# Decoding float64 weights on VectorE alone by a shorter formula, with every split of the experts' weights on VectorE

## The chip, the cores and the metric

The kernel runs on one core of a Trainium2 chip. The metric is device time in microseconds (us) of one execution; less is better. The names of the engines: PE is TensorE (PEld is its weight load), DVE is VectorE, ACT is ScalarE, POOL is GpSimd, SP is SyncE, which here only issues DMAs.

## The reference, cut to what matters

Three layers follow one another: a gated linear attention, a mixture of eight experts in which each token goes to one expert, and a dense feed-forward layer with a leaky ReLU.

```python
# attention, for every batch and head, over S = 768 steps
state = f[:, :, t, :, None] * state + einsum('bhd,bhe->bhde', k[:, :, t], v[:, :, t])
y[:, :, t] = einsum('bhd,bhde->bhe', q[:, :, t], state)
# x: 3072 tokens x 384
expert_idx = argmax(x @ w_gate, axis=1)          # 8 experts
h = maximum(xe @ w1[e], 0.0); ye = h @ w2[e]     # w1: 384 x 1024, w2: 1024 x 384, per expert
out[mask] = gate_w[mask, None] * ye
# dense layer
h = x @ w_in                                     # 384 x 2048, float64
g = maximum(0.01 * h, h)
return (g @ w_out).astype(float32)               # 2048 x 384, float64
```

The weights of the dense layer, w_in and w_out, arrive as float64: they alone are drawn without a cast to float32. The chip's engines compute in float32, so the kernel takes each float64 apart as two 32-bit integer words and builds a float32 value from them.

## The kernel before

**Stages.** The attention runs first and scatters the tokens by expert. The experts follow as nine passes p = 0 to 8 of eight steps each; a step n = 8p + j handles one 128-column block of an expert's first layer and the same block of its second. Pass 0 runs the first 224 tokens of one expert while the attention is finishing, pass 1 runs 256 more of the same expert, and passes 2 to 8 run the other seven experts with room for 464, 440, 420, 408, 396, 384 and 368 tokens. The dense layer comes last: 96 steps of a first product (line 919) and a second one (line 940).

**Products in two parts.** Every float32 operand is split into a high part in the float32r format and the low remainder. `split` (line 132) does that with a ScalarE cast (line 133) and a subtraction on an engine that its caller names (line 134). A product is three matmuls per 128 rows: high by high, high by low, low by high.

**A step of the experts** is written out in the loop over n from line 874 on; the order of this loop is the order of every engine's own queue. In it `m1(n)` issues 9 matmuls of the first layer (line 296), the ReLU cast on ScalarE (line 299) and the low part `hT` on VectorE (line 300). One part of a decode comes next (`decode_on`, line 883), the DMA of weight block n + 3 (`wload`, tile `wraw`, three buffers), and then `m2(n - 1)`, 9 matmuls of the second layer (line 311). In steps 4, 5 and 6 of a pass `m_tr` transposes a third of the next expert's tokens (line 282) and splits them into `xT` (line 286, VectorE). `wsplit(n + 2)` splits the weight block: half 0 is w1's and half 1 is w2's. Half 0 has its subtraction on VectorE and half 1 on GpSimd, by the default `e1=nc.gpsimd`. Another part of a decode closes the step (line 903).

**Decoding.** A block of the float64 weights is 128 x 384 values; there are 16 of w_in and 16 of w_out. `decode(i)` is a generator of four parts, in lines 686 to 711. `decode_all` chains the 32 blocks. `decode_on` places 104 of the 128 parts, which is 26 blocks, in 109 places: two per step from step 16 on, the start of pass 2. The rest, 24 parts, go into the dense layer, two per step. The high word of a float64 is `hw`, the low word `lw`; both are read with a stride of two words. Seven instructions on VectorE make the leading bits `a` and the scaled rest `b`. For w_in a ScalarE cast and two GpSimd instructions turn these into a high and a low part (lines 709 to 711), and for w_out one GpSimd addition makes a float32 value (line 706), which is split later in the dense layer by `wosplit` (line 948, subtraction on GpSimd). The tiles `d_t`, `d_a` and `d_s` have one buffer each, and `raw` has two; the DMA of block i + 1 (`fload`) is issued in the second part of block i.

Of the kernel before, what the change touches and what calls it, by code (L numbers as in the profile page):

```python
# [7 lines left out]
FP32 = mybir.dt.float32  # L8
# [3 lines left out]
U32 = mybir.dt.uint32  # L12
ACTF = mybir.ActivationFunctionType
ALU = mybir.AluOpType
# [17 lines left out]
FB = FF // 128  # L32
# [40 lines left out]
def kernel(  # L73
# [12 lines left out]
    nc = tc.nc  # L86
# [45 lines left out]
    def split(hi, lo, src, eng):  # L132
        nc.scalar.copy(out=hi, in_=src)  # L133
        eng.tensor_tensor(out=lo, in0=src, in1=hi.bitcast(FP32), op=ALU.subtract)  # L134
# [105 lines left out]
    def wload(n, src=None, eng=nc.sync):  # L240
        if src is None:
            p, j = expert_of(n)
            if p == 1 and j < KEPT:
                return
            if p < 2:
                src = wpk[0, SECOND[j] if p else j]
            else:
                if j == 0:
                    e_at[p] = nc.values_load(tab[0:1, ORD, p - 1:p], engines=[SP_E], min_val=0, max_val=NE - 1)
                src = wpk[bass.ds(e_at[p], 1), j].rearrange("o p c -> (o p) c")  # L250
        wraw[n] = mw.tile([128, 768], FP32, tag="wraw", name="wraw")
        eng.dma_start(out=wraw[n], in_=src)

    def wsplit(n, *halves, e1=nc.gpsimd):
        if KF <= n < KF + KEPT and n not in wraw:
            return
        for i in halves or (0, 1):
            r = wraw[n] if i == 0 else wraw.pop(n)
            w = mw.tile([128, 2, 384], FP32R, tag=f"w{i}", name=f"w{i}")
            split(w[:, 0, :], w[:, 1, :], r[:, 384 * i:384 * (i + 1)], e1 if i else nc.vector)  # L260
            wsp.setdefault(n, []).append(w)

    def pieces(rows):
# [51 lines left out]
    def attention():  # L315
        with ExitStack() as st:
# [62 lines left out]
            def load(g, a=0, b=FW + 2 * SEG):  # L379
                for h in range(2):  # L380
                    nc.sync.dma_start(out=fkqb[g % NBUF][64 * h:64 * h + D, a:b], in_=fkq[g, h, :, a:b])

            def load_v(g):
                vt[g] = sb.tile([128, PB, 2, D], FP32, tag="v", name="v", bufs=7)
                nc.sync.dma_start(out=vt[g], in_=v[g])
# [35 lines left out]
            def sc(g):  # L421
                aps[g] = a = [bank(B_A + h, [PB, 128], "A") for h in range(2)]
                for p in range(PB):
                    for h in range(2):
                        r = slice(64 * h, 64 * h + 64)
                        nc.tensor.matmul(out=a[h][:, p, :], lhsT=kh[g][r, cols(p)], rhs=qh[g][r, cols(p)],
                                         start=True, stop=True)
# [10 lines left out]
            def tr(g):  # L438
                t_ps = bank(B_T, [PB, 128], "T")
                for p in range(PB):  # L440
                    nc.tensor.transpose(t_ps[:, p, :], kh[g][:, cols(p)], ident)
                kn[g] = sb.tile([128, PB, 128], FP32, tag="kn", name="kn", bufs=2)
                nc.scalar.copy(out=kn[g], in_=t_ps)
# [53 lines left out]
            def route2(i, n=2):  # L497
                route_b(i, n, bank(B_R, [n, NE], "R"))
# [38 lines left out]
            for g in range(NG):  # L537
                if g + 5 < NG:
                    load(g + 5)
                if g + 3 < NG:  # L540
                    load_v(g + 3)
                if 14 <= g < 17:
                    wload(g - 14)
                if g < 12:
                    for _ in range(2 if g % 3 == 2 else 1):
                        e, r0 = divmod(nz * ZR, GW)
                        nc.sync.dma_start(
                            out=xs[e * NT + r0:e * NT + r0 + ZR, :].rearrange("(p j) d -> p (j d)", p=128), in_=zero)
                        nz += 1
                sc(g)  # L550
                if g % NCH < NCH - 1:
                    tr(g)
                if g + 2 < NG:
                    suffix(g + 2)
                if g == 0:
                    warm_up(WARM2)
                if g + 3 < NG:
                    prep_a(g + 3)
                mask(g)
                if g >= 4:  # L560
                    logits(g - 4)
                if g >= 1 and (g - 1) % NCH < NCH - 1:
                    kv(g - 1)
                if g + 2 < NG:
                    prefix(g + 2)
                if g in (7, 11, 15, 19):
                    route_a(g - 7, 4)
                if g in (21, 23):
                    route_a(g - 5, 2)
                if g in (8, 12, 16, 20):  # L570
                    route2(g - 8, 4)
                    ready += 4
                if g == 22:
                    route2(16)
                    ready += 2
                if g == 1:
                    ys(0)
                if g > 2:
                    ys(g - 2)
                if g == 2:  # L580
                    xo(0)
                if g > 3:
                    xo(g - 3)
                out_to = ngt
                if ngt < ready:
                    gated(ngt, 2)
                    ngt += 2
                if 17 <= g < 23 and g % 2:
                    wsplit((g - 17) // 2, e1=nc.vector)
                if g == 22:  # L590
                    ok1 = check_decay()
                if g == 20:
                    wload(3)
                if g == 21:
                    wload(4)
                for _ in range(2):
                    if g >= 13 and nsc < out_to:
                        scatter(nsc)
                        nsc += 1
# [30 lines left out]
            gated(NG - 2, 2)  # L630
            scatter(NG - 2)
            scatter(NG - 1)
            wsplit(3, 1, e1=nc.vector)
            wload(6)
            e2(1)
            wsplit(4)
# [25 lines left out]
    def experts_and_ffn(place):  # L662
        with ExitStack() as st:
# [4 lines left out]
            wi = [wb.tile([128, 2, 384], FP32R, name=f"wi{i}") for i in range(FB)]  # L668
            wo = [wb.tile([128, 384], FP32, name=f"wo{i}") for i in range(FB)]
# [8 lines left out]

            def decode(i):

                r = raw.pop(i).rearrange("p (n t) -> p n t", t=2)
                lw, hw = r[:, :, 0], r[:, :, 1]
                t = dec.tile([128, 384], I32, tag="d_t", name="d_t")
                a = dec.tile([128, 384], I32, tag="d_a", name="d_a")
                s = dec.tile([128, 384], I32, tag="d_s", name="d_s")
                nc.vector.tensor_scalar(out=t, in0=hw, scalar1=0x7FF00000, scalar2=None, op0=ALU.bitwise_and)  # L686
                nc.vector.tensor_scalar(out=t, in0=t, scalar1=float(896 << 20), scalar2=float(896 << 20),
                                        op0=ALU.max, op1=ALU.subtract)
                nc.vector.tensor_scalar(out=s, in0=hw, scalar1=-0x80000000, scalar2=None, op0=ALU.bitwise_and)  # L689
                yield  # L690
                if 2 <= i + 1 < 2 * FB:
                    fload(i + 1)
                nc.vector.scalar_tensor_tensor(out=a, in0=hw, scalar=0xFFFFF, in1=t,  # L693
                                               op0=ALU.bitwise_and, op1=ALU.bitwise_or)
                nc.vector.scalar_tensor_tensor(out=a, in0=a, scalar=3, in1=s,  # L695
                                               op0=ALU.logical_shift_left, op1=ALU.bitwise_or)
                nc.vector.scalar_tensor_tensor(out=s, in0=t, scalar=3, in1=s,
                                               op0=ALU.logical_shift_left, op1=ALU.bitwise_or)
                yield
                b = t.bitcast(FP32)  # L700
                nc.vector.scalar_tensor_tensor(out=b, in0=lw.bitcast(U32), scalar=2.0 ** -52, in1=s.bitcast(FP32),  # L701
                                               op0=ALU.mult, op1=ALU.mult)
                yield
                af = a.bitcast(FP32)
                if i >= FB:
                    nc.gpsimd.tensor_tensor(out=wo[i - FB], in0=af, in1=b, op=ALU.add)
                else:
                    hi, lo = wi[i][:, 0, :], wi[i][:, 1, :]
                    nc.scalar.copy(out=hi, in_=af)
                    nc.gpsimd.tensor_tensor(out=af, in0=af, in1=hi.bitcast(FP32), op=ALU.subtract)  # L710
                    nc.gpsimd.tensor_tensor(out=lo, in0=af, in1=b, op=ALU.add)
                yield

            def decode_all():
# [342 lines left out]
```

## Time and profile before

| quantity | value |
|---|---|
| median of 3 runs | 836.73 us (836.01 to 838.64) |
| the profiled execution | 834.25 us, its span 832.5 us |
| PE busy | 778.9 us, 94% of the span |
| DVE busy | 548.2 us, 66% |
| ACT busy | 397.2 us, 48% |
| POOL busy | 352.9 us, 42% |
| granted TensorE clock, mean | 0.988 |

The span runs from the first to the last instruction; the profiled execution's own time is 1.75 us more. Busy shares are means over stages that have different limits, so a share of the whole span does not tell what one stage waits for. A matmul's busy time includes its passage through the array, so that a PE that looks fully busy may still be issuing at less than its best rate; the distance between the starts of successive groups of matmuls tells that rate.

### The profile page before, as it was taken

What the parts mean: (1) busy time and instruction counts of PE and PEld (TensorE: products, weight loads), DVE (VectorE), ACT (ScalarE), POOL (GpSimd) and SP (SyncE); (2) the same over time, 40 slices, a digit from 0 to 9 for tenths busy, and PEclk for the clock granted to TensorE, in tenths of its full rate; (3) what the DMA queues carried; (4) which work ended last, traced back from release to release, by engine and by line L of the source; (5) the groups of instructions that cost most, each with busy time, mean ns of one, the idle gap of its engine ahead of it and who ended that gap; (6) DMA issues with size and microseconds to landing.
All of it is one profiled execution on the core that took longest, in us unless ns stands there. A gap on an engine that the chain in (4) does not pass through costs nothing.

```text
span 832.5 us, 14166 instructions
## 1 busy us (share of the span) xinstructions
PE 778.9 (94%) x5201; PEld 705.8 (85%) x5202; DVE 548.2 (66%) x973; ACT 397.2 (48%) x798; POOL 352.9 (42%) x338
## 2 busy tenths in 40 slices
PE   6998988989999998999799999999999999999993
PEld 5777766889898987999789899999999999999993
DVE  7999998675898899999968843433433433343331
ACT  3666775645455444545343444434444444444441
POOL 6221562337676766666533352233224224224222
PEclk9999999999999999999999999999999999999997
DMA  9999941256476764786301010000001001001001
GB/s 188 244 281 313 260 151 40 102 181 199 149 190 131 206 160 126 210 190 152 117 31 44 20 39 1 1 17 21 1 1 39 1 1 38 1 1 39 1 0 43
DMA packets 35024, 81.78 MB, mean 98 GB/s; under 512 B 7904, under 2 KB 15168, under 8 KB 34944
## 3 DMA queue, kind: packets, MB, share of 16 engines
q1 hardware_dynamic: 31104, 71.32, 32.5%
q0 software_dynamic: 3840, 9.45, 3.1%
q8 instruction: 43, 0.70, 0.4%
q14 instruction: 37, 0.30, 0.1%
HBM read 65.02 MB, written 15.74 MB: 97 GB/s over the span
## 4 chain that ended last, share of the span: by engine, by line
PE 58%; DVE 23%; DMA 7%; issue 5%; ACT 3%; POOL 2%; POOLq 0%; SPq 0%; DVEq 0%; ACTq 0%
PE h L919 22%; PE oacc L940 22%; PE acc L311 6%; PE h L296 5%; DMA fkq<-in_fkq 5%; DVE w L134 3%; DVE d_t L686 2%; DVE kh L405 2%; DVE d_s L689 2%; DMA xs<-zero 2%; DVE d_a L695 2%; DVE d_a L693 2%; DVE hT L300 1%; DVE d_t L701 1%; DVE am L433 1%
## 5 line engine op out<-in xcount | busy, mean ns | idle before, releaser
L940 PE MATMUL oacc<-wos,g 128*128 128x384 f32 x1152 | 217.4, 337 | 0.0
L919 PE MATMUL h<-ysp,wi 128*128 128x512 f32 x864 | 213.3, 392 | 0.3 <-DVE t L928 0.3
L134 POOL TENSOR_TENSOR wos<-wo,wos 128x384 fp32r<-128x384 f32 x96 | 100.3, 1045 | 262.4 <-ACT wos L133 262.4
L940 PEld LDWEIGHTS oacc<-wos,g 128*128 128x128 f32 x1152 | 204.7, 188 | 7.8
L919 PEld LDWEIGHTS h<-ysp,wi 128*128 128x128 f32 x864 | 161.1, 188 | 28.3 <-DVE t L928 0.6
L928 DVE TENSOR_TENSOR t<-t,h 128x512 f32<-128x512 f32 (+1 forms) x97 | 66.2, 682 | 145.3 <-ACT t L927 145.3
L311 PE MATMUL acc<-hT,w 128*128 128x224 f32 (+8 forms) x648 | 125.6, 336 | 9.2 <-DVE hT L300 8.7
L296 PE MATMUL h<-xT,w 128*128 128x256 f32 (+7 forms) x576 | 118.2, 347 | 5.9 <-DVE w L134 5.8
L311 PEld LDWEIGHTS acc<-hT,w 128*128 128x128 f32 x648 | 109.1, 189 | 15.7 <-DVE hT L300 12.6
L134 DVE TENSOR_TENSOR g<-t,g 128x512 fp32r<-128x512 f32 (+1 forms) x97 | 66.7, 687 | 66.1 <-PE oacc L940 47.3
L296 PEld LDWEIGHTS h<-xT,w 128*128 128x128 f32 x576 | 98.7, 189 | 12.8 <-DVE w L134 9.8
L927 ACT ACTIVATE t<-h 128x512 f32<-128x512 f32 (+1 forms) x97 | 57.5, 592 | 103.7 <-PE h L919 103.6
L133 ACT CAST g<-t 128x512 fp32r<-128x512 f32 (+1 forms) x97 | 59.8, 617 | 94.0 <-DVE t L928 94.0
L134 POOL TENSOR_TENSOR w<-wraw,w 128x384 fp32r<-128x384 f32 x65 | 73.8, 1136 | 55.6 <-ACT w L133 54.9
L133 ACT CAST w<-wraw 128x384 fp32r<-128x384 f32 x138 | 66.8, 513 | 31.6 <-PE acc L311 23.5
L408 POOL TENSOR_TENSOR kh<-fkq,kh 128x512 f32<-128x512 f32 x24 | 28.6, 1192 | 82.0 <-DVE kh L405 44.6
L134 DVE TENSOR_TENSOR w<-wraw,w 128x384 fp32r<-128x384 f32 x73 | 58.1, 800 | 6.2 <-ACT w L133 6.2
L299 ACT ACTIVATE hT<-h 128x256 fp32r<-128x256 f32 (+7 forms) x64 | 31.9, 499 | 54.4 <-PE h L296 54.1
L133 ACT CAST wos<-wo 128x384 fp32r<-128x384 f32 x96 | 49.1, 512 | 9.1 <-PE oacc L940 0.4
L300 DVE SCALAR_TENSOR_TENSOR hT<-h,hT 128x256 fp32r<-128x256 f32 (+7 forms) x64 | 35.7, 557 | 8.7 <-ACT hT L299 8.7
L483 PE MATMUL X<-cw_sb,yt 128*128 128x104 f32 x192 | 27.6, 289 | 14.1 <-DVE lg L492 8.2
L483 PEld LDWEIGHTS X<-cw_sb,yt 128*128 128x128 f32 x192 | 23.7, 195 | 19.0 <-DVE lg L492 8.9
(139 smaller groups left out, 919.3 us busy)
## 6 DMA issues: line engine op xcount, KB each, us to landing
wraw<-in_wpk SPq DMA_DIRECT2D x69, 384.0 KB, 4.0
fkq<-in_fkq SPq DMA_DIRECT2D x44, 288.9 KB, 8.6
xs<-zero SPq DMA_DIRECT2D x16, 384.0 KB, 8.5
raw<-in_w_in SPq DMA_DIRECT2D x16, 384.0 KB, 3.9
raw<-in_w_out SPq DMA_DIRECT2D x16, 384.0 KB, 3.7
v<-in_v SPq DMA_DIRECT2D x24, 192.0 KB, 8.2
xw<-xs SPq DMA_DIRECT2D x5, 768.0 KB, 5.7
xw<-xs SPq DMA_DIRECT2D x2, 576.0 KB, 6.9
```

What stands on the lines that cost most here:

```text
L133: nc.scalar.copy(out=hi, in_=src)
L134: eng.tensor_tensor(out=lo, in0=src, in1=hi.bitcast(FP32), op=ALU.subtract)
L296: nc.tensor.matmul(out=h_ps, lhsT=w[:, a, kk * 128:(kk + 1) * 128], rhs=xT[p][kk][:, b, :], start=(kk == 0 and a + b == 0), stop=(kk == 2 ...
L299: nc.scalar.activation(out=t[:, 0, :], in_=h_ps, func=ACTF.Relu)
L300: nc.vector.scalar_tensor_tensor(out=t[:, 1, :], in0=h_ps, scalar=0.0, in1=t[:, 0, :].bitcast(FP32), op0=ALU.max, op1=ALU.subtract)
L311: nc.tensor.matmul(out=a_ps[d], lhsT=w[:, a, d * 128:(d + 1) * 128], rhs=t[:, b, :], start=(j == 0 and a + b == 0), stop=(j == KF - 1 and ...
L408: nc.gpsimd.tensor_tensor(out=tokens(kh[g]), in0=chunks(kb[g % NBUF]), in1=tokens(kh[g]), op=ALU.mult)
L483: nc.tensor.matmul(out=x_ps[:, p, :], lhsT=yt[i % 2][:, p, :], rhs=cw_sb[:, p, :], start=True, stop=True)
L919: nc.tensor.matmul(out=h_ps, lhsT=wi[i][:, a, kk * 128:(kk + 1) * 128], rhs=ysp[j][kk][:, b, :], start=(kk == 0 and a + b == 0), stop=(kk ...
L927: nc.scalar.activation(out=t[:, c], in_=h_ps[:, c], func=ACTF.Copy, scale=0.01)
L928: nc.vector.tensor_tensor(out=t[:, c], in0=t[:, c], in1=h_ps[:, c], op=ALU.max)
L940: nc.tensor.matmul(out=oacc[j][s], lhsT=g[:, b, s * 128:(s + 1) * 128], rhs=w[:, a, :], start=(i == 0 and a + b == 0), stop=(i == FB - 1 a ...
```

## The change

All of a block's decoding, apart from one ScalarE cast for w_in, moves to VectorE, by another formula. The absolute bits are floored at a small value and shifted by three places, then masked so that the leading bits of a w_in block fit the high part exactly; sign and top exponent bit are put back by one combined instruction. The bits that the mask cut off (the low nine bits of the high word) and the low word are added up and scaled into the low part directly. The two GpSimd instructions of a w_in block and the one of a w_out block are gone. The argument `e1` of `wsplit` is gone too: both halves' subtractions run on VectorE for every weight block of the experts.

```diff
-    def wsplit(n, *halves, e1=nc.gpsimd):
+    def wsplit(n, *halves):
...
-            split(w[:, 0, :], w[:, 1, :], r[:, 384 * i:384 * (i + 1)], e1 if i else nc.vector)
+            split(w[:, 0, :], w[:, 1, :], r[:, 384 * i:384 * (i + 1)], nc.vector)
...
-                    wsplit((g - 17) // 2, e1=nc.vector)
+                    wsplit((g - 17) // 2)
...
-            wsplit(3, 1, e1=nc.vector)
+            wsplit(3, 1)
...
-                nc.vector.tensor_scalar(out=t, in0=hw, scalar1=0x7FF00000, scalar2=None, op0=ALU.bitwise_and)
-                nc.vector.tensor_scalar(out=t, in0=t, scalar1=float(896 << 20), scalar2=float(896 << 20),
-                                        op0=ALU.max, op1=ALU.subtract)
-                nc.vector.tensor_scalar(out=s, in0=hw, scalar1=-0x80000000, scalar2=None, op0=ALU.bitwise_and)
+                tf = b = t.bitcast(FP32)
+                keep = 0x3FFFF000 if i < FB else 0x3FFFFFF8
+                nc.vector.tensor_scalar(out=t, in0=hw, scalar1=0x7FFFFFFF, scalar2=None, op0=ALU.bitwise_and)
+                nc.vector.tensor_scalar(out=tf, in0=tf, scalar1=2.0 ** -15, scalar2=None, op0=ALU.max)
+                nc.vector.tensor_scalar(out=t, in0=t, scalar1=3, scalar2=keep,
+                                        op0=ALU.logical_shift_left, op1=ALU.bitwise_and)
                 yield
                 if 2 <= i + 1 < 2 * FB:
                     fload(i + 1)
-                nc.vector.scalar_tensor_tensor(out=a, in0=hw, scalar=0xFFFFF, in1=t,
+                nc.vector.scalar_tensor_tensor(out=a, in0=hw, scalar=-0x40000000, in1=t,
                                                op0=ALU.bitwise_and, op1=ALU.bitwise_or)
-                nc.vector.scalar_tensor_tensor(out=a, in0=a, scalar=3, in1=s,
-                                               op0=ALU.logical_shift_left, op1=ALU.bitwise_or)
-                nc.vector.scalar_tensor_tensor(out=s, in0=t, scalar=3, in1=s,
-                                               op0=ALU.logical_shift_left, op1=ALU.bitwise_or)
+                nc.vector.tensor_scalar(out=s, in0=a, scalar1=-0x800000, scalar2=None, op0=ALU.bitwise_and)
                 yield
-                b = t.bitcast(FP32)
-                nc.vector.scalar_tensor_tensor(out=b, in0=lw.bitcast(U32), scalar=2.0 ** -52, in1=s.bitcast(FP32),
-                                               op0=ALU.mult, op1=ALU.mult)
+                low, af = lw.bitcast(U32), a.bitcast(FP32)
+                if i < FB:
+                    nc.scalar.copy(out=wi[i][:, 0, :], in_=af)
+                    nc.vector.tensor_scalar(out=t, in0=hw, scalar1=0x1FF, scalar2=None, op0=ALU.bitwise_and)
+                    nc.vector.scalar_tensor_tensor(out=b, in0=t, scalar=2.0 ** 32, in1=low,
+                                                   op0=ALU.mult, op1=ALU.add)
+                    low = b
                 yield
-                af = a.bitcast(FP32)
+                nc.vector.scalar_tensor_tensor(out=wi[i][:, 1, :] if i < FB else b, in0=low, scalar=2.0 ** -52,
+                                               in1=s.bitcast(FP32), op0=ALU.mult, op1=ALU.mult)
                 if i >= FB:
-                    nc.gpsimd.tensor_tensor(out=wo[i - FB], in0=af, in1=b, op=ALU.add)
-                else:
-                    hi, lo = wi[i][:, 0, :], wi[i][:, 1, :]
-                    nc.scalar.copy(out=hi, in_=af)
-                    nc.gpsimd.tensor_tensor(out=af, in0=af, in1=hi.bitcast(FP32), op=ALU.subtract)
-                    nc.gpsimd.tensor_tensor(out=lo, in0=af, in1=b, op=ALU.add)
+                    nc.vector.tensor_tensor(out=wo[i - FB], in0=af, in1=b, op=ALU.add)
                 yield
```

## Rows read from the trace of the kernel before

**Rows 1.** Windows: us; busy PE, PEld, DVE, ACT, POOL; PEclk, DMA share, GB/s.

```profile
203.75:232.26 28.51, 28.51 (x141) 25.07 (x139) 24.76 (x42) 13.73 (x30) 18.97 (x18) 1.00 0.55 170
...
296.10:329.27 33.17, 30.41 (x158) 27.51 (x157) 32.76 (x49) 15.86 (x35) 22.39 (x21) 1.00 0.61 167
...
386.80:418.66 31.86, 27.21 (x154) 25.38 (x154) 29.42 (x45) 13.19 (x28) 18.04 (x16) 1.00 0.44 123
482.00:800.00 318.00, 318.00 (x1604) 289.71 (x1603) 124.19 (x177) 141.43 (x253) 99.76 (x98) 1.00 0.04 13
```

**Rows 2.** Timeline of PE: start, us, engine, line, operation, shape, count.

```profile
218.80 0.69 PE L282 MATMUL xt<-c_sb,xw 128*128 128x128 f32 x4
219.41 2.15 PE L296 MATMUL h<-xT,w 128*128 128x464 f32 x9
221.41 2.04 PE L311 MATMUL acc<-hT,w 128*128 128x464 f32 x9
223.28 0.69 PE L282 MATMUL xt<-c_sb,xw 128*128 128x128 f32 x4
...
379.88 0.48 PE L282 MATMUL xt<-c_sb,xw 128*128 128x128 f32 x3
380.13 1.81 PE L296 MATMUL h<-xT,w 128*128 128x384 f32 x9
...
393.57 1.66 PE L296 MATMUL h<-xT,w 128*128 128x368 f32 x9
395.07 1.66 PE L311 MATMUL acc<-hT,w 128*128 128x368 f32 x9
```

**Rows 3.** Waits from 204 to 420 us: us in total, times, longest.

```profile
POOL w L134 <- ACT w L133: 40.7, 29, 3.4
...
ACT w L133 <- PE acc L311: 20.7, 23, 2.1
PEld acc L311 <- DVE hT L300: 9.9, 10, 1.7
PEld h L296 <- DVE w L134: 9.8, 12, 1.7
```

**Rows 4.** Timeline of pass 5: a GpSimd subtraction and three decode instructions.

```profile
299.20 1.33 POOL L134 TENSOR_TENSOR w<-wraw,w 128x384 fp32r<-128x384 f32 x1
...
299.59 1.17 DVE L686 TENSOR_SCALAR d_t<-raw 128x384 int32<-128x384 int32 x1
...
300.79 0.36 DVE L687 TENSOR_SCALAR d_t<-d_t 128x384 int32<-128x384 int32 x1
...
301.06 0.35 DVE L689 TENSOR_SCALAR d_s<-raw 128x384 int32<-128x384 int32 x1
```

**Rows 5.** Lines and tiles alone: ns minimum/median/maximum, first and last start.

```profile
L686 DVE TENSOR_SCALAR d_t<-raw x32: 360/1168/1189, 205.3 to 472.7; 128x384 int32<-128x384 int32 x32
L701 DVE SCALAR_TENSOR_TENSOR d_t<-raw,d_s x32: 543/552/2441, 210.4 to 478.7; 128x384 f32<-128x384 uint32 x32
L134 DVE TENSOR_TENSOR w<-wraw,w x73: 540/559/2820, 115.8 to 413.8; 128x384 fp32r<-128x384 f32 x73
L300 DVE SCALAR_TENSOR_TENSOR hT<-h,hT x64: 424/566/640, 185.0 to 416.4; 128x256 fp32r<-128x256 f32 x8, 128x464 fp32r<-128x464 f32 x8, 128x440 fp32r<-128x440 f32 x8, 128x420 fp32r<-128x420 f32 x8
L133 ACT CAST w<-wraw x138: 496/514/536, 115.3 to 409.3; 128x384 fp32r<-128x384 f32 x138
```

**Rows 6.** Timeline of pass 0's last steps.

```profile
170.03 2.82 DVE L134 TENSOR_TENSOR w<-wraw,w 128x384 fp32r<-128x384 f32 x1
...
175.67 1.15 PE L311 MATMUL acc<-hT,w 128*128 128x224 f32 x8 [1.60 <-DVE hT L300]
```

**Rows 7.** The chain that ended last, early in the dense layer.

```profile
450.00 2.12 PE oacc L940 x12
...
479.75 2.11 PE oacc L940 x12
...
483.92 2.10 PE oacc L940 x12
```

## The prediction

> **What bounds the kernel now.** I read the windows by stage first, to find where PE is short of work. From 482 us on, inside the dense layer, PE is busy all of the time at full clock with DVE at 124 of 318 us [rows 1]: nothing on VectorE can shorten that stretch, and the change reaches it only in its first 60 us. The attention has no line that the change touches, apart from splits that were on VectorE already. What is left is passes 2 to 8 of the experts, from 203.75 to 418.66 us, that is 214.9 us [rows 1] (seven windows, one a pass, of which three stand there).
>
> Busy PE does not show there how much is lost, so I took the distance between the starts of groups of nine matmuls where nothing waits. At 464 columns it is 223.28 - 221.41 = 1.87 us, at 368 it is 395.07 - 393.57 = 1.50 [rows 2]; between them I go linearly, 0.00385 us per column, which makes 1.78, 1.70, 1.65, 1.61 and 1.56 for 440, 420, 408, 396 and 384. A transposition of four tiles costs 0.61 and makes the group after it 2.00 instead of 1.87, so 0.74; one of three costs 0.25 [rows 2], with some 0.1 on the group behind it 0.35. A step without waits is two groups and 3/8 of a transposition: 4.02, 3.84, 3.68, 3.59, 3.35, 3.25 and 3.00 us in passes 2 to 8. Eight of each are 197.8 us, and the stretch begins one group late: 196.0. So 214.9 - 196.0 = 18.9 us are lost to waits. The waits say on whom: PE's weight loads wait for hT and for w, both from DVE, 9.9 and 9.8 us [rows 3]. And DVE is full in the passes that lose: 32.76 of 33.17 us in pass 5, 29.42 of 31.86 in pass 8, against 24.76 of 28.51 in pass 2, where PE does not wait [rows 1].
>
> **Why DVE is full.** Its durations in isolation are 0.36 us for a one-input instruction, 0.55 for a two-input one (0.552), 0.56 for a split and 0.57 for hT [rows 4, 5]; xT I take as hT. There are 104/109 decode parts in a place and two places in a step, 1.91 parts, or 0.477 blocks. The old block is 3 x 0.36 + 4 x 0.55 = 3.28 us, so a step is hT 0.57, one split 0.56, 3/8 of an xT 0.21 and 0.477 x 3.28 = 1.56: 2.90 us. Measured in pass 5 are 32.76 / 8 = 4.10 [rows 1]. The missing 1.20 us per step is the lengthening that rows 4 show: GpSimd's subtraction runs from 299.20 to 300.53, the decode instruction that starts at 299.59 lasts 1.17 and ends 0.23 after it, and the next ones, with GpSimd quiet, take 0.36 and 0.35. The median of that line is 1168 ns with a minimum of 360, and the other lines have maxima of 2441 and 2820 [rows 5]. So GpSimd's two-input work is paid for by VectorE.
>
> **The change, part by part.**
>
> Splits: the second half's subtraction adds 0.56 to a step on DVE.
>
> Decode: a w_in block is five one-input and three two-input instructions, 5 x 0.36 + 3 x 0.55 = 3.45 us; a w_out block four, two and an addition at a split's price, 1.44 + 1.10 + 0.56 = 3.10. Floor, shift-and-mask and mixed-integer multiply-add have no row; the nearest are the decode's own lines of the same kind and size, and I take those. The bounds: nothing cheaper than 0.35, and at worst each one-input instruction at the two-input price, 0.19 more.
>
> GpSimd: one split, and two instructions or one per block, leave. It keeps the scatters of indices and, in pass 8, three splits of the dense layer's input. The lengthening should go with them: I take 0 left in passes 2 to 7.
>
> The new step on DVE is 0.57 + 1.12 + 0.21 + 1.65 = 3.55 us while w_in is decoded (33 of the steps, to the start of pass 6), 3.38 while w_out is, and at most 0.57 + 0.84 + 1.48 = 2.9 in pass 8, whose last two steps split nothing. Against PE's 4.02, 3.84, 3.68, 3.59, 3.35, 3.25 and 3.00 it is short only by 0.03 in pass 6 and 0.13 in pass 7, 1.3 us in all. Two things shift that. Independent neighbours overlap: 301.06 follows 300.79 by 0.27, not by 0.36 [rows 4]. Uneven steps work the other way: the first two parts of a block are about twice the last two. I take 2.5 us left of 18.9, with 0 and 5 as its ends: a gain of 16.4.
>
> A wait is added: the second half's subtraction stands in VectorE's queue, and its ScalarE cast can't start before m2(n - 1) has freed the buffer (20.7 us of casts waited for acc [rows 3]). Behind it wait one decode part and hT(n + 1), for which m2(n + 1) waits. With T the start of step n and C a group, the cast ends at T + 2C + 0.6 (the cast is 0.51 [rows 5]). DVE gets there after hT(n), which ends at T + C + 1.1, a part at about 0.85 and the first split: T + C + 2.5. That is later for any C below 1.9, so I cost the wait at nothing. The cover is DVE's own load, and without it the price is in the third rival.
>
> The DMA of weights is next to be late. A freed wraw buffer now depends on DVE alone. A w_out block frees `raw` one part later than before, and SP holds the weight loads behind that DMA. The loads move 167 GB/s at a share of 0.61 [rows 1], which at 8% less time is 0.66; I cost it at nothing, and it is part of the 2.5.
>
> Pass 0's end: VectorE's split of 2.82 us, 2.26 over its price, and PE's wait of 1.60 for hT [rows 6] come of the same lengthening; four splits at 0.56 take its place. Between 0 and 1.6 I take 1.0, because the splits give back 2.2 of what several lengthened instructions lose.
>
> The dense layer's start: from 450.00 to 479.75 seven pairs take 29.75 us; at 483.92 - 479.75 = 4.17 they would be 29.2 [rows 7]. The 0.56 lost is DVE's first two decode parts, which shrink from 3 x 0.36 + 3 x 0.55 = 2.73 to 4 x 0.36 + 0.55 = 1.99; the last two grow from 0.55 to 1.1, in steps where DVE has room. I take 0.4.
>
> Sum: 16.4 + 1.0 + 0.4 = 17.8 us. The profiled execution's 834.25 would be 816.5. The median, 836.73, is 2.5 above it; from there 818.9, say 819.
>
> **A rule that speaks against it.** DVE is the fullest engine after PE in pass 5 [rows 1], and the change gives it more to do. The Trainium skill, "Perfetto Trace Analysis", section "Optimizing Scalar/DVE Operations", says that with DVE saturated, handing work to ScalarE or even GpSimd may make sense; it adds that this may not help between VectorE and GpSimd, which share a read port. By its first half the change goes the wrong way, and the time is that of the fourth rival, 868; by rows 4 it goes the right way and the time is 819. I go by the row.
>
> **The rivals.**
>
> 1. As forecast, PE sets the pace: 815 to 823.5. Chance 0.74.
>
> 2. VectorE, or the weight loads behind it, stays the bound in the late passes. If every one-input instruction cost the two-input price, a step would be 0.45 longer with w_in and 0.36 with w_out: 4.00 and 3.74. The shortfalls are then 0, 0.16, 0.32, 0.41, 0.4, 0.5 and about 0.2, some 16 us, and the gain 4: 833. With half of that, 826. For it: there is 0.1 us or less to spare from pass 5 on. Against it: decode lines alike in kind agree within 0.01. Range 823.5 to 833, chance 0.16.
>
> 3. The wait for the cast comes to VectorE. On GpSimd it was 40.7 us in 29 waits [rows 3]. Taken over whole, 40.7 / 56 = 0.73 per step lifts 3.5 to 4.2, over the present 214.9 / 56 = 3.84: 56 x 0.4 = 22 us slower, 859. It decides from 0.35 us per step on. Against it: GpSimd waited because it had little else to do. Chance 0.04 for any loss by it.
>
> 4. The lengthening isn't GpSimd's, and the change does not do what it says: VectorE stays at 4.1 and gets 0.56 more, 56 x 0.56 = 31 us: 868. It decides where a step on DVE passes 3.84. Against it: rows 4. Chance 0.03.
>
> 5. Gain and losses cancel, within 0.3% of before (2.5 us, about what a measurement of this kernel can tell from no change). Chance 0.03.
>
> **How the numbers follow.** Faster is rivals 1 and 2, 0.90; same 0.03; slower 0.07. The low end is the whole 18.9 + 1.6 + 0.56 = 21.1 us off, 815.6, less a little for the runs' own spread, 814.5. From there to 823.5 lies 0.74; up to 826.5 I take in 0.06 of rival 2, which makes 0.80.
>
> **What the profile after would show.** Right: passes 2 to 8 in 197 to 202 us; DVE's first decode line at a median near 0.36 us, splits without maxima over 1.5 us before the dense layer; PE's waits for hT and w under 5 us together; POOL nearly idle from 204 to 400 us. Wrong: DVE lines that stay long without GpSimd work beside them; one-input lines near 0.55; idle time on DVE put down to the ScalarE cast of w; casts that wait for wraw with PE idle behind them.

## The result, and the profile after

The changed kernel takes 839.32 us in the median of 20 runs (836.54 to 846.32), the one before 835.51 (20 runs): a ratio of 1.0051, 95% interval 1.0037 to 1.0065. It is slower by half a per cent where 819 us was forecast. The profiled execution is the longest of the 20, 846.32 us with a span of 844.5, so it shows the loss larger than the median does: 12.0 us against the span of before.

The page of the kernel after: busy time of each engine, then three rows of its 40 slices of 21 us.

```profile
PE 784.1 (93%) x5201; PEld 713.5 (84%) x5202; DVE 526.3 (62%) x1054; ACT 396.6 (47%) x798; POOL 225.0 (27%) x225
...
POOL 6222553374400000000122233224224224224222
PEclk8999998998889999999999999999999999999997
DMA  9999941269886466556611100001001001001001
```

GpSimd has a third less to do, as was meant, and stands still from the twelfth slice on until the dense layer is near. But in slices 10 to 12, about 190 to 253 us, the granted clock is below 9 tenths, and the DMA engines are 8 to 9 tenths busy. Windows of the kernel after, first passes 1 and 2, then passes 3 to 8 (columns as in [rows 1]):

```profile
183.16:261.62 78.46, 59.42 (x306) 52.07 (x305) 36.18 (x79) 25.92 (x60) 23.84 (x24) 0.87 0.84 116
261.62:431.19 169.57, 168.82 (x929) 162.90 (x927) 149.73 (x330) 88.30 (x191) 4.88 (x4) 1.00 0.57 179
```

The same two stretches of the kernel before:

```profile
183.29:232.26 48.97, 48.97 (x306) 45.34 (x304) 34.25 (x61) 25.88 (x60) 32.77 (x31) 1.00 0.56 178
232.26:418.66 186.40, 173.77 (x928) 161.66 (x927) 173.21 (x271) 89.01 (x191) 121.32 (x107) 1.00 0.65 163
```

This is the whole story in four lines. Passes 3 to 8 became 16.8 us shorter: PE is busy in 168.82 of 169.57 us, and VectorE has idle time again. Passes 1 and 2, which had no wait before, became 29.5 us longer. The dense layer is 0.5 us shorter (844.5 - 431.19 against 832.5 - 418.66) and all before pass 1 is 0.1 shorter: +29.5 - 16.8 - 0.5 - 0.1 = +12.1, which is the span's difference of 12.0 within rounding.

Timeline of the kernel after, at the first long wait of PE; the idle time before an instruction and what ended it stand in brackets.

```profile
194.38 1.24 PE L311 MATMUL acc<-hT,w 128*128 128x256 f32 x9
195.46 0.56 PE L282 MATMUL xt<-c_sb,xw 128*128 128x128 f32 x4
...
200.90 0.93 ACT L133 CAST w<-wraw 128x384 fp32r<-128x384 f32 x2 [6.87 <-DMA wraw<-in_wpk]
201.44 1.03 DVE L134 TENSOR_TENSOR w<-wraw,w 128x384 fp32r<-128x384 f32 x2 [6.74 <-ACT w L133]
201.46 2.46 PE L296 MATMUL h<-xT,w 128*128 128x256 f32 x9 [5.44 <-ACT w L133]
...
214.74 3.85 PE L296 MATMUL h<-xT,w 128*128 128x464 f32 x9 [5.72 <-ACT w L133]
218.39 2.12 PE L311 MATMUL acc<-hT,w 128*128 128x256 f32 x9
```

The chain reads from top to bottom of the brackets: a weight block lands late, its cast waits, VectorE and PE wait for the cast. Six waits of PE between 195 and 252 us add up to 18.9 us: five for the cast of a weight block, 16.0 us, and one of 2.9 us for the load of the next expert's tokens. The rest of the 29.5, some 10 us, is the clock: after such waits the granted clock falls, 0.87 over the stretch. The group at 214.74 takes 218.39 - 214.74 = 3.65 us where the same group takes 1.87 without a wait [rows 2], and the clock of just that window is the lower level, 1.2 GHz instead of 2.4:

```profile
214.74:218.39 3.65, 3.65 (x9) 3.11 (x10) 1.71 (x4) 1.55 (x4) 2.84 (x3) 0.50 1.23 196
```

DMA issues from 183 to 252 us in the kernel after: KB each and median us from issue to landing.

```profile
wraw<-in_wpk SPq DMA_DIRECT2D x12, 384.0 KB, 15.8
raw<-in_w_in SPq DMA_DIRECT2D x4, 384.0 KB, 17.3
...
ids<-tok,posi POOLq DMA_INDIRECT x24, 16.8
```

And in the kernel before, the same stretch:

```profile
wraw<-in_wpk SPq DMA_DIRECT2D x19, 384.0 KB, 3.5
raw<-in_w_in SPq DMA_DIRECT2D x7, 384.0 KB, 3.5
...
ids<-tok,posi POOLq DMA_INDIRECT x6, 4.0
```

All 24 index scatters (`ids_out`, each 128 rows of 4 bytes) now fall into this stretch, six did before, and a weight block takes 15.8 us to land instead of 3.5. The tile `ids` alone, after (ns minimum/median/maximum, first and last start):

```profile
L126 POOL DMA_INDIRECT ids<-tok,posi x24: 970/972/1261, 183.1 to 227.3; - x24
```

and before:

```profile
L126 POOL DMA_INDIRECT ids<-tok,posi x24: 990/1102/1132, 206.4 to 386.6; - x24
```

Nothing in the program says when an index scatter is issued, apart from its place in GpSimd's queue. There it stood between GpSimd's splits and decode instructions, which waited for ScalarE and VectorE and so kept it in step with n, one every two steps. With those gone GpSimd finds nothing to wait for and issues all 24 within 44 us. It starts at 183.1 us, with pass 1, a whole pass ahead of the first scatter's place in the order of steps, which is the first step of pass 2.

### The profile page after: what moved, and what is told of

It is laid out like the page before. It is cut to its first block, busy times and chain, and to the rows that moved or that the text cites. A ratio compares the mean times of both kernels' runs of the same rounds, so it can differ in the third digit from the quotient of the medians.

```text
span 844.5 us, 14045 instructions
## 1 busy us (share of the span) xinstructions
PE 784.1 (93%) x5201; PEld 713.5 (84%) x5202; DVE 526.3 (62%) x1054; ACT 396.6 (47%) x798; POOL 225.0 (27%) x225
## 4 chain that ended last, share of the span: by engine, by line
PE 69%; DMA 14%; DVE 10%; issue 3%; ACT 2%; POOL 0%; SPq 0%; DVEq 0%; POOLq 0%; ACTq 0%
PE h L922 23%; PE oacc L943 23%; PE acc L311 10%; PE h L296 10%; DMA wraw<-in_wpk 7%; DMA fkq<-in_fkq 4%; DMA v<-in_v 2%; DVE w L134 2%; DVE kh L405 2%; DVE am L433 1%; DVE qh L417 1%; DMA cw_sb<-in_cw 1%; PE xt L282 1%; PE X L483 1%; ACT yt L478 1%
## 5 line engine op out<-in xcount | busy, mean ns | idle before, releaser
L296 PE MATMUL h<-xT,w 128*128 128x256 f32 (+7 forms) x576 | 121.4, 356 | 16.3 <-ACT w L133 16.0
L296 PEld LDWEIGHTS h<-xT,w 128*128 128x128 f32 x576 | 102.7, 196 | 22.4 <-ACT w L133 17.3
L311 PEld LDWEIGHTS acc<-hT,w 128*128 128x128 f32 x648 | 112.7, 195 | 7.8 <-DVE w L134 2.2
L134 DVE TENSOR_TENSOR w<-wraw,w 128x384 fp32r<-128x384 f32 x138 | 72.3, 561 | 44.6 <-ACT w L133 44.3
L134 POOL TENSOR_TENSOR ysp<-y,ysp 128x512 fp32r<-128x512 f32 x3 | 3.9, 1290 | 189.6 <-ACT ysp L133 187.8
L483 PE MATMUL X<-cw_sb,yt 128*128 128x104 f32 x192 | 27.9, 291 | 12.9 <-DVE lg L492 10.3
```

The costliest lines, as they stand in the source:

```text
L296: nc.tensor.matmul(out=h_ps, lhsT=w[:, a, kk * 128:(kk + 1) * 128], rhs=xT[p][kk][:, b, :], start=(kk == 0 and a + b == 0), stop=(kk == 2 ...
L311: nc.tensor.matmul(out=a_ps[d], lhsT=w[:, a, d * 128:(d + 1) * 128], rhs=t[:, b, :], start=(j == 0 and a + b == 0), stop=(j == KF - 1 and ...
L483: nc.tensor.matmul(out=x_ps[:, p, :], lhsT=yt[i % 2][:, p, :], rhs=cw_sb[:, p, :], start=True, stop=True)
```

## The experiments

Theory: the index scatters run ahead on an idle GpSimd, and their burst holds up the weight loads. Rival A: the weight buffers come free too late, or the loads outrun the DMA queues by themselves. Rival B: the granted clock falls first. Ratios are against the kernel before on the same chip.

**Scatters paced.** Each scatter's positions come from a copy that ScalarE makes at the scatter's own place:

```diff
+    pose = const.tile([128, NG], I32, name="pose")
...
             def ids_out(i, key="ids"):
-                scatter_rows(key, ids[:, :], posi[:, i:i + 1], tok[:, i:i + 1], NT - 1)
+                at = posi
+                if key == "ids":
+                    nc.scalar.copy(out=pose[:, i:i + 1], in_=posi[:, i:i + 1])
+                    at = pose
+                scatter_rows(key, ids[:, :], at[:, i:i + 1], tok[:, i:i + 1], NT - 1)
```

> Changed kernel, but each of the 24 index scatters reads its positions from a copy that ScalarE makes at the scatter's own place in the step order, so GpSimd can't issue it earlier. Theory (the scatters run ahead on an idle GpSimd and hold up the weight loads): index DMAs spread over 204 to 400 us, weight loads land in about 4 us, no ScalarE wait for wraw over 2 us, passes 2 to 8 in 197 to 203 us, 816 to 823 us in all. Rival A (weight buffers come free too late, or the loads outrun the DMA queues by themselves): nothing changes, 836 to 842. Rival B (the granted clock falls first and the rest follows): nothing changes either, and the clock is 0.8 to 0.9 around 200 to 250 us again.

Measured: 817.03 us, ratio 0.9803 (0.9777 to 0.9828). The tile `ids`, and the two stretches in windows:

```profile
L127 POOL DMA_INDIRECT ids<-tok,pose x24: 969/1128/1242, 204.4 to 372.3; - x24
```

```profile
182.23:231.19 48.96, 48.96 (x306) 45.27 (x305) 35.85 (x79) 26.28 (x64) 5.43 (x5) 1.00 0.57 185
231.19:400.82 169.63, 168.89 (x929) 162.98 (x927) 150.03 (x330) 90.33 (x211) 27.22 (x24) 1.00 0.69 179
```

Passes 1 and 2 are back at 48.96 us at full clock and passes 3 to 8 keep the whole gain. Rivals A and B, which said that nothing would change, fall: the loads, VectorE's order and the buffers are those of the changed kernel.

**The burst moved.** All 24 scatters at step 40, the first held back by one ScalarE copy:

```diff
+                if key == "ids" and i == 0:
+                    nc.scalar.copy(out=pose[:, i:i + 1], in_=posi[:, i:i + 1])
...
-                if n >= 2 * KF and n % 2 == 0 and n // 2 - KF < NG:
-                    ids_out(n // 2 - KF)
+                if n == 5 * KF:
+                    for i in range(NG):
+                        ids_out(i)
```

> Changed kernel with all 24 index scatters put at step 40, the start of pass 5, and held back until then by one ScalarE copy. Theory: passes 1 to 4 run without a wait, and the burst takes its toll in pass 5 to 6: index DMAs and weight loads land late (8 us and more) from about 290 to 340 us, 15 to 30 us are lost there, 833 to 845 in all. Rival A: the loss stays at 195 to 252 us, where it was.

Measured: 832.57 us (828.62 to 835.11), 0.9968 (0.9950 to 0.9985), just under the stated 833 to 845; the scatters start between 296.7 and 335.3 us, and weight blocks issued from 296 to 352 us land in 12.4 us. Windows before, at the beginning of and after the moved burst's start:

```profile
181.51:229.93 48.42, 48.42 (x303) 44.80 (x302) 35.32 (x78) 25.91 (x60) 0.75 (x1) 1.00 0.56 184
290.00:319.00 29.00, 29.00 (x159) 28.20 (x158) 25.22 (x56) 14.03 (x32) 15.73 (x15) 1.00 0.83 160
319.00:352.00 33.00, 25.29 (x114) 20.48 (x113) 17.16 (x39) 11.66 (x27) 9.09 (x9) 0.95 0.82 138
```

The loss went where the burst went: none in passes 1 and 2, and PE short of work from 319 us on, some 20 us behind the first scatter. By the medians it is 15 us, less than the 22 at the old place.

**Half a burst.** Twelve scatters left free to run ahead, twelve moved into the dense layer's first six steps.

```diff
-                if n >= 2 * KF and n % 2 == 0 and n // 2 - KF < NG:
+                if n >= 2 * KF and n % 2 == 0 and n // 2 - KF < NG // 2:
...
+                    if key == "out" and n < NG // 4:
+                        ids_out(NG // 2 + 2 * n)
+                        ids_out(NG // 2 + 2 * n + 1)
...
```

> Changed kernel with 12 of the 24 index scatters free to run ahead as they do now, and 12 in the dense layer. Theory: the loss grows with the scatters in the burst; with half of them some 10 us of the 22 are left, lost between 195 and 225 us: 825 to 830. If it were one late load that sets the whole loss, 836 to 840, and if a few scatters cost nothing, 817.

Measured: 831.13 us (827.85 to 834.68), 0.9965 (0.9947 to 0.9984), just above the stated 825 to 830. Windows of passes 1 and 2, and of the dense layer:

```profile
184.75:246.09 61.34, 52.81 (x306) 48.14 (x304) 36.02 (x79) 26.00 (x60) 11.91 (x12) 0.94 0.72 148
415.68:831.70 416.02, 400.94 (x2017) 363.94 (x2016) 176.73 (x265) 174.95 (x316) 137.05 (x131) 0.99 0.06 16
```

Twelve free scatters cost 61.34 - 48.97 = 12.4 us in passes 1 and 2, where 24 cost 29.5, each in one profiled execution. Another 2.7 us are lost in the dense layer, 416.02 us instead of 413.3, to the twelve that were moved there: VectorE waits 4.8 us for a late load of float64 weights. The loss grows with the burst, and neither one late load nor a free first dozen explains it.

**No scatters in the experts.** All 24 go into the dense layer, two in each of its first 12 steps, the index table's load behind them.

```diff
-                if n >= 2 * KF and n % 2 == 0 and n // 2 - KF < NG:
-                    ids_out(n // 2 - KF)
-                if n == 2 * (KF + NG):
-                    ids_in()
...
+                    if key == "out" and n < NG // 2:
+                        ids_out(2 * n)
+                        ids_out(2 * n + 1)
+                    if key == "out" and n == NG // 2:
+                        ids_in()
```

> Changed kernel with the 24 index scatters moved into the dense layer, two in each of its first 12 steps, the load of the index table behind them; no instruction is added. Theory: as with pacing, and the experts' loads are alone: passes 2 to 8 in 196 to 202 us, the dense layer as before since its DMA queues are idle and GpSimd has 3 us of room per step: 815 to 822. Rival A: 836 to 842.

Measured: 817.33 us, 0.9787 (0.9771 to 0.9803), the same as with pacing. Here the scatters run beside four loads of float64 weights and nothing else. DMA queues (packets, MB, share of the 16 engines' time) and the issues of the dense layer's first 56.7 us, q1 being SP's queue and q0 the scatters':

```profile
q1 hardware_dynamic: 576, 1.57, 37.0%
q0 software_dynamic: 768, 0.01, 1.0%
raw<-in_w_out SPq DMA_DIRECT2D x4, 384.0 KB, 10.3
```

and of the same stretch in the changed kernel, which has no scatters there:

```profile
q1 hardware_dynamic: 576, 1.57, 9.0%
raw<-in_w_out SPq DMA_DIRECT2D x4, 384.0 KB, 3.0
```

So the scatters slow loads without any help from the experts' traffic: the same 576 packets take four times as long, 37.0% instead of 9.0%, while the scatters' own packets take 1.0%. It costs nothing in this run, because the dense layer does not wait for these loads (413.3 us from its first matmul on, as in the changed kernel).

The same move made in the kernel before is the control:

> The kernel before, with the 24 index scatters moved into the dense layer as in the other runs. Theory: they were spread out and cost next to nothing there, VectorE stays full: 833 to 836. If the scatters cost the experts time even when spread, as a rival has it, part of the 18 us gained by moving them shows here too: 820 to 830.

Measured: 838.23 us, 1.0041 (1.0027 to 1.0055): slower, outside what was expected. The move by itself is therefore no gain. It takes 7.7 us more after the experts (836.6 - 415.07 against 832.5 - 418.66): the chain from 440 to 500 us goes through the scatters on GpSimd for 23.6% of its time, and GpSimd there still has the old decode's additions beside its splits. The experts themselves are 4.8 us shorter (415.07 - 184.54 against 418.66 - 183.29), so that spread scatters were not quite free either. In the changed kernel paced scatters cost nothing there: passes 3 to 8 take 169.63 us with them and 169.59 without. That speaks for GpSimd's time, of which the changed kernel has more to spare, and against the DMA queues, but no run separates the two.

**Each part alone.** The decode alone is the changed kernel with the second halves on GpSimd again (the argument `e1` comes back); the splits alone is the kernel before, old decode and all, with this line edited the other way:

```diff
...
-            split(w[:, 0, :], w[:, 1, :], r[:, 384 * i:384 * (i + 1)], nc.vector)
+            split(w[:, 0, :], w[:, 1, :], r[:, 384 * i:384 * (i + 1)], e1 if i else nc.vector)
...
```

> The decode's part of the change alone: the second halves of the weights are split on GpSimd again, which waits for each block's cast. Theory: that wait keeps the index scatters in step, weight loads land in about 4 us; VectorE has 3.0 us of its own work per step and some 0.5 of lengthening by one GpSimd subtraction, under PE's 3.0 to 4.0 in most passes: 818 to 826. Rival A: as the changed kernel, some waits for wraw, 830 to 840.

> The splits' part alone: both halves on VectorE, the old decode with its GpSimd instructions. Theory: the decode's GpSimd instructions, which wait for VectorE, keep the index scatters in step from pass 2 on, so no burst; VectorE has 0.56 more per step and loses the lengthening by one GpSimd instruction of about two per step: 3.46 us of its own work and some 0.5 of lengthening, against the 4.1 of before and PE's 3.0 to 4.0: 822 to 834. Rival A (the moved splits by themselves free weight buffers late): waits for wraw of over 5 us, 836 and more.

Measured: the decode alone 819.49 us, 0.9813 (0.9797 to 0.9830); the splits alone 825.27, 0.9877 (0.9850 to 0.9905), both as expected. Either part alone is a gain, and either leaves GpSimd something to wait for. The tile `ids` of the two runs, in this order:

```profile
L126 POOL DMA_INDIRECT ids<-tok,posi x24: 989/995/1126, 208.0 to 376.2; - x24
L126 POOL DMA_INDIRECT ids<-tok,posi x24: 972/1127/1179, 185.8 to 380.1; - x24
```

In the second run one scatter goes early, at 185.8 us, and the next one waits behind a decode until 216.7. Weight blocks issued from 183 to 252 us land in 3.7 and 4.4 us. Only both parts together let GpSimd run free. The two runs also separate who lengthens VectorE's instructions. The first decode instruction with the splits on GpSimd, decode off it:

```profile
L692 DVE TENSOR_SCALAR d_t<-raw x32: 344/1145/1245, 206.9 to 459.6; 128x384 int32<-128x384 int32 x32
```

and with the decode's instructions on GpSimd, splits off it:

```profile
L686 DVE TENSOR_SCALAR d_t<-raw x32: 342/349/1183, 209.3 to 465.3; 128x384 int32<-128x384 int32 x32
```

So it was the split on GpSimd that made this line 1168 ns [rows 5], and not GpSimd's decode instructions.

**Zero fills held back.** In the profiled execution of the kernel after, pass 0's end gained nothing; there GpSimd ran ahead too. The eight zero fills of `y`, one a step before, are issued together. Timeline after:

```profile
174.65 8.25 POOL L901 MEMSET y<- 128x1164 f32 x8 [4.28 <-DMA wraw<-in_wpk]
...
175.18 1.57 DVE L214 TENSOR_SCALAR pos_t<-pos_t 128x8 f32<-128x8 f32 x1
...
177.89 1.15 PE L311 MATMUL acc<-hT,w 128*128 128x224 f32 x8 [2.06 <-DVE w L134]
```

The version with no scatters in the experts has the same fills:

```profile
177.22 8.26 POOL L901 MEMSET y<- 128x1164 f32 x8 [4.19 <-DMA wraw<-in_wpk]
...
177.84 0.48 DVE L214 TENSOR_SCALAR pos_t<-pos_t 128x8 f32<-128x8 f32 x1
...
179.46 1.16 PE L311 MATMUL acc<-hT,w 128*128 128x224 f32 x8 [0.96 <-DVE w L134]
```

The instruction ends 2.10 us behind the start of the fills in the first trace and 1.10 in the second. A fill takes 8.25 / 8 = 1.03 us, so it ends just behind the second fill or the first, and what is lost depends on where in a fill it falls. On top of this second version, one small GpSimd copy of the positions' last result goes ahead of the fills; what is left of the positions is issued in step 8 at once for that, which leaves the order of VectorE's instructions there as it was:

```diff
+                if n == KF:
+                    for _ in place:
+                        pass
+                    nc.gpsimd.tensor_copy(out=idx[:, 0:2], in_=bad)
                 if n < 2 * KF:
-                    next(place, None)
```

> The kernel with the index scatters in the dense layer, and the eight zero fills of GpSimd held back until VectorE has worked out the positions, by one two-element copy on GpSimd. Theory: the zero fills, run together at about 175 us, lengthen the one-input instructions of the positions (1.57 and 1.00 us instead of 0.16) and with them PE's wait of 1.0 to 2.1 us for a split; without them the wait is 0.3 or less, 1 to 1.5 us gained: 815.5 to 817. Rival: the wait is for the weight block or for VectorE's own work, no change from 817.

Measured: 814.98 us, 0.9776 (0.9755 to 0.9797), just under the stated 815.5 to 817. Timeline of the same places:

```profile
175.65 0.16 DVE L214 TENSOR_SCALAR pos_t<-pos_t 128x8 f32<-128x8 f32 x1
...
176.04 1.56 PE L311 MATMUL acc<-hT,w 128*128 128x224 f32 x9
...
177.44 1.17 PE L296 MATMUL eh<-xT,w 128*128 128x224 f32 x9
```

The instruction is back at 0.16 us, and PE's wait at that group is gone from the line; the longest wait left near it is 0.33 us, one group later, which is 0.36 in the other two traces. From the group's start to the next group's is 177.44 - 176.04 = 1.40 us, 2.22 in the version that it starts from (178.23 to 180.45) and 3.32 in the kernel after (175.56 to 178.88). So the trace shows the mechanism, worth 0.8 us here; the 2.3 us between the two medians come from different chips, each beside its own kernel before, and their intervals overlap, so that a gain of that size is not shown. It is the fastest version measured, 2.2% under the kernel before and 2.9% under the changed one by medians.

## Why the prediction was wrong

**What bounds the kernel, and why VectorE is full: right.** Passes 3 to 8 run at PE's pace once GpSimd's subtractions are gone, and VectorE's lines are at their isolated price. Tile and line views of the kernel after:

```profile
L692 DVE TENSOR_SCALAR d_t<-raw x32: 346/352/1182, 225.7 to 485.4; 128x384 int32<-128x384 int32 x32
L694 DVE TENSOR_SCALAR d_t<-d_t x32: 359/360/365, 226.5 to 487.0; 128x384 int32<-128x384 int32 x32
L707 DVE SCALAR_TENSOR_TENSOR d_t<-d_t,raw x16: 558/559/562, 234.4 to 357.5; 128x384 f32<-128x384 int32 x16
```

The forms without a row, shift-and-mask and the mixed-integer multiply-add, cost what the nearest lines had promised, 0.36 and 0.56 us; rival 2's dearer instructions did not come.

**The terms of the sum, where the burst is kept away: right in size.** With paced scatters the experts from pass 1 on take 218.6 us instead of 235.4, a gain of 16.8 where 16.4 stood; the dense layer gains 0.5 where 0.4 stood. That profiled execution takes 816.18 us, where the sum gave 816.5, but 1.1 us of it were gained ahead of pass 1 (182.23 instead of 183.29), which is partly luck, as the next paragraph shows. The added wait for the cast, costed at nothing, was nothing: VectorE's splits waited for it 5.0 us in all, and PE only 0.7 us in pass 8, for other work of VectorE. So rival 3 did not come, nor rival 4.

**Pass 0's end, 1.0 us: the reason was incomplete.** The lengthening by splits went, and the lengthening by zero fills came in its place. In the kernel after PE's longest wait there is 2.06 us instead of 1.60 [rows 6]. In the runs with scatters paced, moved, and in the dense layer, whose instructions up to there are the same, it is 1.25, 1.08 and 0.96, by where the fills happened to fall.

**The step that failed** is the paragraph on the DMA of weights, "I cost it at nothing", together with the sentence that GpSimd "keeps the scatters of indices". I counted what leaves GpSimd, and what stays, but not when the instructions that stay would now be issued. The argument about the loads was made with their own number alone, 167 GB/s at a share of 0.61, as if the index DMAs kept their places. The runs put in its place: 24 scatters in 44 us, weight blocks landing in 15.8 us instead of 3.5, 18.9 us of waits on PE and some 10 more at the lower clock in the profiled execution, against a gain of 17. By the medians the burst costs 22 us (839.32 - 817.03). All of the forecast's chance for a slower kernel stood on other mechanisms, though its list of signs of being wrong named the one that came: casts that wait for `wraw` with PE idle behind them.

The late loads come through a queue that the change does not touch: SP issues them, GpSimd the scatters. The Trainium skill, "DMA: Bandwidth & Descriptors", section "Issuing engines are not separate DMA queues", says that DMAs of all issuing engines run on the same 16 DMA engines and interleave. The traces agree: 15.8 us for an SP load during GpSimd's burst, 3.5 without. But the time that the scatters' own packets take does not explain it, at 1.0% where the loads' packets went from 9.0% to 37.0%. What holds the loads up stays open: why rows of 4 bytes weigh so much was not tried, and no run here changes their size.

## What to carry to other kernels

Before work is taken off an engine, read what else stands in that engine's queue and ask what kept it in its place: an instruction that waits sets the pace of everything behind it, DMAs above all. If later instructions were paced only by it, give them a dependency of their own, or move them to where neither their traffic nor their time on the engine holds anything up. A load that was never late is judged with all that can be in the DMA queues at once, and not by its own bandwidth.

## What the runs showed of the hardware that was not expected

- A burst of small scatters slows large loads of another queue: 24 scatters of 128 rows of 4 bytes, some 12 KB in all, cost 22 us by the medians. With only four loads beside them, these landed in 10.3 us instead of 3.0.
- A GpSimd instruction that only writes lengthens VectorE as well: beside zero fills of 128 x 1164, a one-input instruction on 8 elements took 1.57 us in one trace and 0.48 in another, ending just behind a fill both times, and 0.16 without.
- Waits of PE cost more than themselves: 18.9 us of waits, the longest 5.7, came with a granted clock of 0.87 over 78 us, and a group at half its rate, at 0.50.
